# Where the weight sums of a gated feed-forward stage stand in VectorE's queue

## The chip, the cores and the metric

The kernel runs on one core of a Trainium2 chip. The metric is the device time of one execution in microseconds: 1489.54 us before the change, the median of three runs (1488.31 to 1489.56). The profiled execution has a span of 1488.6 us, with the TensorE clock granted in full.

## What is computed

Four layers on a sequence of 2048 tokens of width 1024: linear attention, gated feed-forward, and both once more with the same weights, each behind a layer norm and with a residual. The change lies in the feed-forward layer:

```python
x = x + _A_ref(_layernorm(x), A_wqkv, A_wo)              # linear attention, 32 heads
x = x + _B_ref(_layernorm(x), B_W_gate, B_W_up, B_W_down)
# _B_ref:
gate = einsum("bsd,df->bsf", x, W_gate)                  # d = 1024, f = 3584
up = einsum("bsd,df->bsf", x, W_up)
gate = gate * (gate > 0)
return einsum("bsf,fd->bsd", gate * up, W_down)
```

## The kernel before

The attention layers are `layer_A` (l = 0 and 2), the feed-forward layers `layer_B` (l = 1 and 3). A feed-forward layer goes over two chunks c of 1024 tokens. In each chunk, 14 units u (256 of the 3584 hidden columns) pass through `glu`, and then `down` multiplies the hidden tiles by W_down.

`glu` forms the gate and up products of a unit as 2 x 2 blocks with seven block products where eight would be needed. The price of that is sums of blocks: of the tokens (`sums_x`) and of the weights (`make_gu`, lines 680, 682 and 683: one instruction of 128 x 1024 and two of 128 x 512 for each of gate and up, so six for a unit). Both are formed on VectorE. A product (`mm`, line 742) is four matmuls into a PSUM bank; seven products for gate and seven for up make 56 matmuls a unit. Between them VectorE and ScalarE move partial results: v is product 5, copied by ScalarE to m5 (line 759); x is product 1, copied by ScalarE into y (line 763) and then completed by product 2; y takes product 6, is read by VectorE for z = y + m5 (line 773: zg and zu), takes product 7, is read again for m5 = y + m5 (line 776), and takes product 4. The matmuls that add to y must wait until VectorE has read it. The finished gate is clipped by ScalarE (line 750, r), and VectorE multiplies gate and up into the hidden tile h (`put`, line 753), three times a unit; GpSimd does the fourth product (line 780). The last of the three, h<-yu,r, is the last VectorE instruction of the unit's own, and `self.last_put` holds it.

The weight sums are made once, in chunk 0 of layer 1 (`first`), and written to memory (line 684, a DMA issued on ScalarE's queue) for the later three chunks, which load them (line 673). In this chunk, unit u's call in `layer_B` does this before `glu`: it lets the ring of weight tiles load up to five tiles ahead of unit u's gate weight (line 670, on SyncE's queue), and puts the sums of unit u+1 on the list of later tasks, due at the fourth tick, that is after four products of unit u. The sums of unit 0 are made in `layer_A`, near its end. All weight tiles, hidden tiles and token tiles share one pool of 16 slots, so a load may have to wait until an earlier weight tile has been used.

What order the instructions have on an engine is decided by the program order together with a scheduler, which may move an instruction ahead of others on its engine where its data allow it. `behind` limits that: with `self.tc.issue_after(it)` the instructions made inside stand after `it` in their engine's queue. This adds no semaphore. Before the change `it` is `self.last_x`, the last residual addition of the attention layer (line 564), which is long past; so all the sums may stand as early as the scheduler places them. In the built program they are mostly in groups of four weights (12 instructions), in every second unit.

Of the kernel before, what the change touches and what calls it, by code (L numbers as in the profile page):

```python
# [89 lines left out]
class _Net:  # L90
# [770 lines left out]
    def layer_B(self, l, final):  # L861
        ring = self.ring

        def behind(it, fn):
            with self.tc.issue_after(it.ins):
                fn()

        for c in range(2):
            hT = []
            first = l == 1 and c == 0  # L870
            for u in range(self.U):
                if u % 2 == 0:
                    hT.append(self.slot(f"h{l}_{c}_{u // 2}", dtype=F16))
                ring.load_to(ring.index((l, c, "g", u)) + 5)
                if first:
                    if u + 1 < self.U:
                        self.later.at(4, lambda u=u: behind(self.last_x, lambda: [
                            self.make_gu(ring.get((l, c, w, u + 1)), w, u + 1) for w in "gu"]))
                self.glu(l, c, u, hT)
                if c == 0 and u == (self.U - 1 if first else 0):  # L880
                    after = self.last_put.ins
            if c == 0:
                self.ln_chunk(l, 1, 20, 3, 3, after)
            elif not final:
                self.ln_later(l + 1, 0, 28, 6, 4)
            self.down(l, c, hT, final)
# [68 lines left out]
```

## Time and profile before

| stage or engine | figure |
|---|---|
| span of the profiled execution | 1488.6 us |
| first gated chunk: first product to first down product | 237.22 to 411.08 us |
| one undisturbed unit of it (unit 2: 262.08 to 274.17) | 12.09 us |
| TensorE matmul busy, whole span | 1474.4 us |
| VectorE busy, whole span | 836.7 us |
| VectorE busy, 297 to 309 us and 309 to 321 us | 9.65 and 5.46 us |
| weight sums: L680, L682, L683 (28 each), median | 682, 419, 418 ns |
| landing of a weight load (L670): least, median, most | 3.6, 4.9, 10.4 us |

In a timeline row the columns are start and duration in us, engine, line, operation, output<-input, shape, count, and in brackets how long the engine was idle before and what ended that. PE is TensorE, DVE is VectorE, ACT is ScalarE, POOL is GpSimd, SPq SyncE's queue. A row of a wait gives who waited for whom, the total in us, how often, and the longest. Matmul rows overlap: four matmuls are shown with 1.03 us, and follow each other at 0.864 us.

### The profile page before, as it was taken

How to read it: one execution, taken by the hardware profiler on the slowest of the kernel's cores; microseconds unless marked ns; L12 is line 12 of the kernel's file. 1: busy time of each engine (PE TensorE's matmuls, PEld its weight loads, DVE VectorE, ACT ScalarE, POOL GpSimd, SP SyncE). 2: the span in 40 equal slices, each digit the busy share in tenths (PEclk: the TensorE clock that was granted, in tenths of full speed). 3: DMA queues.
4: the chain of work that ended last, by engine and by line, in shares of the span. 5: the costliest groups of instructions: out<-in, count | busy, mean ns of one | idle time of the engine just before them, and what ended most of it. 6: DMA issues, size and time to landing. Idle time of an engine off the chain costs nothing.

```text
span 1488.6 us, 18556 instructions
## 1 busy us (share of the span) xinstructions
PE 1474.4 (99%) x6993; PEld 670.5 (45%) x7039; DVE 836.7 (56%) x1427; ACT 508.6 (34%) x911; POOL 277.1 (19%) x190
## 2 busy tenths in 40 slices
PE   9999999999999999999999999999999999999999
PEld 4444444444444444444444444444444444444444
DVE  8995789565494533346366555874345433444632
ACT  5752323333330233340057513333332203333300
POOL 1356540110000011110023492401111000111000
PEclk9999999999999999999999999999999999999999
DMA  9856539443458954445723038494343688444461
GB/s 282 215 167 177 114 60 260 155 170 127 145 174 230 344 179 130 150 133 189 221 43 71 29 52 253 87 283 142 129 151 132 188 240 276 142 142 143 150 209 43
DMA packets 313753, 242.91 MB, mean 163 GB/s; under 512 B 105280, under 2 KB 290880, under 8 KB 312768
## 3 DMA queue, kind: packets, MB, share of 16 engines
q1 hardware_dynamic: 303696, 221.41, 50.9%
q10 hardware_dynamic: 9968, 20.32, 3.6%
q8 instruction: 55, 0.90, 0.3%
q14 instruction: 34, 0.28, 0.1%
HBM read 186.65 MB, written 30.41 MB: 146 GB/s over the span
## 4 chain that ended last, share of the span: by engine, by line
PE 85%; DVE 5%; DMA 2%; issue 1%; ACT 0%; DVEq 0%
PE dy L826 10%; PE yu L742 10%; PE yg L742 10%; PE ps L430 8%; PE ps L465 7%; PE dv L826 6%; PE dx L826 6%; PE xu L742 6%; PE xg L742 6%; PE zu L742 3%; PE zg L742 3%; PE vu L742 3%; PE vg L742 3%; PE ps L557 2%; DVE x L564 1%; DVE stats L154 1%
## 5 line engine op out<-in xcount | busy, mean ns | idle before, releaser
L742 PEld LDWEIGHTS <-w 128*128 128x128 f16 (+1 forms) x3136 | 306.6, 98 | 375.8 <-issue 4.6
L430 PE MATMUL ps<-w,xnT 128*128 128x512 bf16 x1024 | 223.9, 379 | 0.5 <-DVE pq L380 0.2
L780 POOL TENSOR_TENSOR h<-m5u,m5g 128x512 f16<-128x512 f32 x56 | 71.2, 1271 | 815.4 <-DVE m5u L776 774.5
L826 PEld LDWEIGHTS <-h 128*128 128x128 f16 x1120 | 109.6, 98 | 132.2
L773 DVE TENSOR_TENSOR zg<-yg,m5g 128x512 f32<-128x512 f32 x56 | 39.1, 699 | 210.9 <-PE yg L742 210.9
L430 PEld LDWEIGHTS <-xnT 128*128 128x128 bf16 x1024 | 99.4, 98 | 120.9 <-issue 2.7
L742 PE MATMUL yg<-s,w 128*128 128x512 f16 x448 | 115.1, 379 | 3.6 <-DVE zg L773 3.6
L742 PE MATMUL xu<-xnT,w 128*128 128x512 f16 x448 | 115.0, 379 | 0.0
L742 PE MATMUL xg<-xnT,w 128*128 128x512 f16 x448 | 115.0, 379 | 0.0
L742 PE MATMUL yu<-s,w 128*128 128x512 f16 x448 | 115.0, 379 | 0.0
L557 PE MATMUL ps<-T,pqT 128*128 128x512 bf16 x500 | 110.4, 379 | 1.4 <-DVE x L564 0.8
L750 ACT ACTIVATE m5g<-m5g 128x512 f32<-128x512 f32 x56 | 35.3, 630 | 202.0 <-DVE m5g L776 187.6
L826 PE MATMUL dy<-w,h 128*128 128x512 f16 x448 | 98.0, 379 | 0.0
L826 PE MATMUL dx<-w,h 128*128 128x512 bf16 x436 | 96.7, 379 | 0.6
L511 POOL TENSOR_TENSOR kvc<-pq,kvc 128x1024 f32<-128x1024 bf16 x32 | 68.1, 2129 | 81.5 <-DVE den L516 70.4
L154 DVE BATCH_NORM_STATS2 stats<-x 128x6 f32<-128x512 f32 (+1 forms) x120 | 76.5, 672 | 1.9 <-DMA x<-in_A_x_dram 1.6
L557 PEld LDWEIGHTS <-pqT 128*128 128x128 bf16 x512 | 49.9, 98 | 61.4 <-issue 1.5
L161 ACT ACTIVATE rstd<-mv,eps 128x1 f32<-128x1 f32 x64 | 18.2, 290 | 163.2 <-DVE mv L159 163.1
L447 POOL TENSOR_TENSOR kvc<-kvc,slab 128x512 f32<-128x512 f32 x46 | 57.1, 1249 | 78.8 <-DVE slab L380 61.0
L759 ACT ACTIVATE m5g<-vg 128x512 f32<-128x512 f32 x56 | 33.4, 597 | 100.6 <-PE vg L742 73.9
L826 PEld LDWEIGHTS <-e 128*128 128x128 f16 x448 | 43.8, 98 | 52.9
L776 DVE TENSOR_TENSOR m5u<-yu,m5u 128x512 f32<-128x512 f32 x56 | 38.7, 691 | 50.7 <-PE yu L742 50.7
(105 smaller groups left out, 1941.0 us busy)
## 6 DMA issues: line engine op xcount, KB each, us to landing
w<-in_B_W_gate_dram SPq DMA_DIRECT2D x56, 512.0 KB, 6.0
w<-in_B_W_up_dram SPq DMA_DIRECT2D x56, 512.0 KB, 4.6
w<-td SPq DMA_DIRECT2D x32, 896.0 KB, 4.6
w<-in_B_W_down_dram SPq DMA_DIRECT2D x24, 896.0 KB, 5.1
w<-tg SPq DMA_DIRECT2D x42, 512.0 KB, 6.9
w<-tu SPq DMA_DIRECT2D x42, 512.0 KB, 6.0
w<-in_A_wqkv_dram SPq DMA_DIRECT2D x10, 1024.0 KB, 8.2
wd<-in_B_W_down_dram SPq DMA_DIRECT2D x7, 1024.0 KB, 7.2
```

What stands on the lines that cost most here:

```text
L154: self.nc.vector.bn_stats(out=stats[:, c, :], in_=src[:, c * fmax:(c + 1) * fmax])
L430: nc.tensor.matmul(by_row(ps), lhsT=self.xnT[l, l_q][:, kt, j * P:(j + 1) * P], rhs=w[:, kt, :].rearrange("p (b i d) -> p i b d", i=R, d=H ...
L447: nc.gpsimd.tensor_tensor(out=ksum[:, cols], in0=ksum[:, cols], in1=pk, op=ALU.add)
L465: nc.tensor.matmul(ps, lhsT=self.xn[l, t][:, d * P:(d + 1) * P], rhs=self.pk[l, t][:, h * NW:(h + 1) * NW], start=(t == 0), stop=(t == sel ...
L511: nc.gpsimd.tensor_tensor(out=prod, in0=pq_of[sc, j], in1=zrow, op=ALU.mult)
L557: nc.tensor.matmul(ps, lhsT=pqT[sc][:, g, j * P:(j + 1) * P], rhs=T[g // 4][:, g % 4, n2 * NW:(n2 + 1) * NW], start=(g == 0), stop=(g == G ...
L742: nc.tensor.matmul(ps, lhsT=W[w][m][:, k, :], rhs=A[m][:, k, :], start=start and k == 0, stop=k == 3, skip_group_check=True)
L750: nc.scalar.activation(out=out, in_=ps, func=ACT.Relu)
L773: nc.vector.tensor_tensor(out=Z[w], in0=Y[w], in1=V[w], op=ALU.add)
L776: nc.vector.tensor_tensor(out=V[w], in0=Y[w], in1=V[w], op=ALU.add)
L780: nc.gpsimd.tensor_tensor(out=h[:, 3, :], in0=V["u"], in1=V["g"], op=ALU.mult)
L826: nc.tensor.matmul(banks[j], lhsT=A(k)[:, j * P:(j + 1) * P], rhs=w[:, i, :], start=start and k == 0, stop=k == self.U - 1, skip_group_che ...
```

## The change

The sums of unit u+1 are placed behind the latest product `self.last_put` where there is one, instead of behind the attention layer's last addition. The name is looked up when the task runs, in unit u after four of its products, when the latest such product is the third of unit u-1 (h<-yu,r). For u = 0 there is none yet in this chunk, and the sums of unit 1 stay behind `last_x`. It is meant to keep VectorE's queue from being filled with sums that are not yet needed.

```diff
                 if first:
                     if u + 1 < self.U:
-                        self.later.at(4, lambda u=u: behind(self.last_x, lambda: [
+                        self.later.at(4, lambda u=u: behind(self.last_put if u else self.last_x, lambda: [
                             self.make_gu(ring.get((l, c, w, u + 1)), w, u + 1) for w in "gu"]))
```

## The prediction

> **What bounds the kernel now.** I read the page first. TensorE is busy for 1474.4 of 1488.6 us, so nothing but TensorE's order and its gaps can move the end.
>
> ```profile
> PE 1474.4 (99%) x6993; PEld 670.5 (45%) x7039; DVE 836.7 (56%) x1427; ACT 508.6 (34%) x911; POOL 277.1 (19%) x190
> ```
>
> The changed lines belong to one stage, the first gated chunk. Its first product starts at 237.22 us and the down product's first (dx) at 411.08. I asked that stage for its waits, TensorE first and then VectorE (columns: engine, line, releaser, us in total, times, longest).
>
> ```profile
> PE yg L742 <- DVE zg L773: 3.6, 2, 2.1
> PE vg L742 <- DVE w L680: 0.2, 1, 0.2
> ```
>
> ```profile
> DVE w L680 <- DMA w<-in_B_W_gate_dram: 4.1, 2, 2.4
> DVE w L680 <- DMA w<-in_B_W_up_dram: 2.8, 2, 1.9
> ```
>
> TensorE waits twice for VectorE's zg, and VectorE itself sat waiting for weight loads in front of its weight sums. The timeline of unit 11 (units counted from 0) shows how the two hang together:
>
> ```profile
> 371.88 0.37 SPq L670 DMA_DIRECT2D w<-in_B_W_gate_dram  x1
> 372.74 0.37 SPq L670 DMA_DIRECT2D w<-in_B_W_up_dram  x1
> ...
> 375.96 0.69 DVE L680 TENSOR_TENSOR w<-w 128x1024 f16<-128x1024 bf16 x1 [2.38 <-DMA w<-in_B_W_gate_dram]
> ...
> 378.59 1.03 PE L742 MATMUL yu<-s,w 128*128 128x512 f16 x4
> 379.45 0.69 DVE L680 TENSOR_TENSOR w<-w 128x1024 f16<-128x1024 bf16 x1 [1.88 <-DMA w<-in_B_W_up_dram]
> 380.18 0.43 DVE L682 TENSOR_TENSOR w<-w 128x512 f16<-128x512 bf16 x1
> 380.64 0.43 DVE L683 TENSOR_TENSOR w<-w 128x512 f16<-128x512 bf16 x1
> 380.98 0.69 DVE L773 TENSOR_TENSOR zg<-yg,m5g 128x512 f32<-128x512 f32 x1
> ...
> 381.73 0.81 PE L742 MATMUL yg<-s,w 128*128 128x512 f16 x3 [2.11 <-DVE zg L773]
> ```
>
> The sums at 375.96 and 379.45 are those of unit 13, two units ahead of use; their weights were asked for only at 371.88 and 372.74, when unit 10 gave its slots back. zg of unit 11 stands behind them in VectorE's queue. It was ready at about 378 and ran at 380.98, and the next matmul of yg, which overwrites what zg reads, waited. Unit 9 has the same picture: the sums of unit 12 run at 353.22, zg at 354.75, yg at 355.50.
>
> [...] zg waited behind a sum that it does not need. [...] at 371.70 an L682 took 0.83 us beside GpSimd's 1.27 us product at 370.98, against a median of 419 ns. [...] 682 ns for 1024 elements, against 0.69 for 512 out of PSUM. Since the trace has all durations, I use its own.
>
> **The change, part by part.** Nothing is added or removed: 84 sum instructions (L680, L682, L683, 28 each) and 28 write-backs (L684) stay. What moves is the place on VectorE of the sums of units 2 to 13. Each block of six now stands after the product h<-yu,r (put 2) of the unit two before it, and so before zg of the unit one before it. In the built order of the changed kernel the blocks are one per unit, where they were mostly four weights in a row every second unit. No semaphore is added: in the built program the first sum waits for its load alone, and order in the queue does the rest. What is queued behind a block is zg, and TensorE's yg waits for zg; so I cost the block against that gap.
>
> First, the room. Take unit 2, which has no sums in its first half:
>
> ```profile
> 262.08 1.03 PE L742 MATMUL vg<-s,w 128*128 128x512 f16 x4
> 262.35 0.69 DVE L753 TENSOR_TENSOR h<-yu,r 128x512 f16<-128x512 f32 x1 [1.03 <-PE yu L742]
> ...
> 267.53 0.70 DVE L773 TENSOR_TENSOR zg<-yg,m5g 128x512 f32<-128x512 f32 x1 [4.49 <-PE yg L742]
> ```
>
> VectorE is idle for 4.49 us, from 263.04 to 267.53. The block needs, from the medians of the tile view,
>
> ```profile
> L680 DVE TENSOR_TENSOR w<-w x28: 677/682/1096, 238.6 to 379.5; 128x1024 f16<-128x1024 bf16 x28
> ```
>
> 2 x 0.68 + 4 x 0.42 = 3.04 us. That fits with 1.4 us to spare. With the longest durations seen (L680 1.10, L682 0.84, L683 0.43) it is 2 x (1.10 + 0.84 + 0.43) = 4.74 us, 0.25 late; but zg then ends at about 268.5 and yg is not due before 268.99. So the upper bound is hidden too. Besides, GpSimd's product (260.53 to 261.80 here) is over by then, so I take the median.
>
> Second, whether the weights are there. The block of unit u+1 now runs about 1 us after unit u starts. Units 10 to 12 are the tight ones. The last weights of unit 12 are asked for at 360.87, those of unit 13 at 372.74; less the gain below, 359.2 and 371.1. Unit 11 starts at 372.55 and unit 12 at about 387.1; less the gain, 370.9 and 383.0. Adding 1 us, the lead is 12.7 and 12.9 us. The landing times of L670 are 3.6/4.9/10.4 (least, median, most). Hence no block should wait for a load.
>
> Third, write-backs. L684 issues on ScalarE's queue and stands between m5u and yu there, waiting for L683 of the gate weight. Counting from a unit's start: put 2 ends at 0.96, two L680, two L682 and one L683 bring 3.6 at the latest, the issue itself 0.33, so 3.9. ScalarE's yu<-xu was at 265.74, or 3.66. It slips by up to 0.3 us; the matmul that needs it, xu's second pass, is at 5.18, yu's at 6.05. Cost 0. A write-back now lands some ten us into the unit before its slot's last use, a whole unit before the next load wants the slot. Cost 0. Two loads (w16, w17) no longer wait for a write-back and may start some 6 us earlier, at 237 to 239; nothing needs them before unit 2. Cost 0. One matmul of the next unit's vg is placed inside every unit instead of some; its sum and bank are ready 3 us before. Cost 0.
>
> Now what goes away. Four matmuls of a product take 0.864 us in the chain of waits. Unit 9: yu at 352.95 + 0.864 = 353.81, yg at 355.50, a gap of 1.69. Unit 11: 378.59 + 0.864 = 379.45 to 381.73, a gap of 2.28. Unit 0 has a small one: the sums of unit 2's gate weight push m5g (L776) to 245.81, and yg goes on at 246.55 instead of 246.31; with m5g ready at about 245.65, some 0.17 comes back. Sum: 1.69 + 2.28 + 0.17 = 4.14 us. As a check, 14 units of 12.09 us (262.08 to 274.17) are 169.3, the stage takes 173.86, so 4.6 us is all that can be had; the 0.4 left is unit 0's own first sums, whose place does not change. After the stage the built orders agree, and its triggers hang on TensorE, so the shift should reach the end whole: 1489.54 - 4.14 = 1485.40 us.
>
> **Rivals.** (a) Half: the stall of unit 11 returns because unit 13's loads land late, or a block's tail delays zg a little. For it: DMA was busy 0.54 to 0.75 in those windows. Against: the 12 us of lead. Time 1489.54 - 1.69 - 0.17 = 1487.7. (b) No change: the 4 us come back as waits in the down product or the second chunk, whose loads have slots freed in the same order. Against: after 411 us TensorE's matmuls wait for 0.7 us in all, and the loads shift with the stage. Time 1489.5. (c) Slower: the blocks are in front of zg in twelve units. If each ran d longer than the room, the time is 1489.5 - 4.1 + 12 d; d = 0.6 gives 1492.6. [...] Against: the room is 1.4 us and a further 0.7 before yg is due.
>
> **How the numbers follow.** Forecast 0.82, (a) 0.07, (b) 0.07, (c) 0.04. The limits of 0.2% are 1486.6 and 1492.5. The forecast's time is uncertain by the 0.4 us of unit 0 and the 1.3 us between the runs of before, so it lies at 1484 to 1486.5 and counts as faster; (a) and (b) are within 0.2%. Faster 0.82, same 0.14, slower 0.04. The range runs from 1484.0 to 1487.7, which takes in (a) and leaves out (b), (c) and a little below.
>
> **What would show it.** Right: in the changed trace L680's waits for DMA and the two waits of yg for zg are gone, a block of six follows each h<-yu,r and ends about 1.4 us before zg, and dx starts near 406.9. Wrong: new waits of yg for zg in many units (c), an L680 still waiting for a load at unit 12 (a), or dx at 407 and new TensorE waits later (b).

## The result, and the profile after

The changed kernel takes 1485.78 us (median of six runs, 1484.59 to 1486.82). The kernel before takes 1489.71 us (median of six, the three named above and three more, 1488.31 to 1490.74). The ratio is 0.9973, with a 95% interval of 0.9961 to 0.9986, so the difference is clear of the noise. The forecast was 1485.40 us, and faster by its limit of 0.2%. The measured difference is 0.27%, with an interval of 0.14 to 0.39%.

On the page, TensorE is busy for almost as long as before, in a span of 1483.6 us where it was 1488.6:

```profile
PE 1473.4 (99%) x6993; PEld 670.5 (45%) x7039; DVE 833.1 (56%) x1427; ACT 508.8 (34%) x911; POOL 276.6 (19%) x190
```

These are the waits of TensorE in the first gated chunk (engine, line, releaser, us in total, times, longest). Of the two rows of before only the small one is left:

```profile
PE vg L742 <- DVE w L680: 0.2, 1, 0.2
```

VectorE's waits in that chunk follow. Before, there were two rows in which L680 waited for a DMA, 6.9 us together. There is none now. VectorE's zg waits for TensorE in 13 of 14 units; before, it did so in 10:

```profile
DVE zg L773 <- PE yg L742: 32.3, 10, 4.5
```

And after:

```profile
DVE zg L773 <- PE yg L742: 25.3, 13, 4.3
DVE h L753 <- PE yu L742: 13.8, 14, 1.0
```

The timeline of unit 11, the place of the longer stall before, now reads:

```profile
369.54 0.37 SPq L670 DMA_DIRECT2D w<-in_B_W_gate_dram  x1
370.40 0.37 SPq L670 DMA_DIRECT2D w<-in_B_W_up_dram  x1
370.48 0.69 DVE L753 TENSOR_TENSOR h<-yu,r 128x512 f16<-128x512 f32 x1 [1.03 <-PE yu L742]
...
371.09 1.28 DVE L680 TENSOR_TENSOR w<-w 128x1024 f16<-128x1024 bf16 x2
...
372.29 0.75 DVE L682 TENSOR_TENSOR w<-w 128x512 f16<-128x512 bf16 x2
...
372.96 0.75 DVE L683 TENSOR_TENSOR w<-w 128x512 f16<-128x512 bf16 x2
...
373.78 0.58 ACT L763 ACTIVATE yu<-xu 128x512 f32<-128x512 f32 x1 [0.40 <-DVE w L683]
...
375.44 0.70 DVE L773 TENSOR_TENSOR zg<-yg,m5g 128x512 f32<-128x512 f32 x1 [1.73 <-PE yg L742]
376.25 1.03 PE L742 MATMUL yu<-s,w 128*128 128x512 f16 x4
...
377.12 1.03 PE L742 MATMUL yg<-s,w 128*128 128x512 f16 x4
```

The loads at 369.54 and 370.40 are those of unit 13, asked for, as before, when unit 10 gave its slots back. But the six sums at 371.09 to 373.71 are now those of unit 12, whose weights were asked for a unit earlier. VectorE then sits idle for 1.73 us until TensorE has filled yg, zg runs at 375.44, and the next yg follows yu at 377.12, one product (0.87 us) later, without a gap. Unit 9 has the same picture, with zg at 351.27 and yg at 352.94.

The first down product, dx, starts here:

```profile
406.25 2.11 PE L826 MATMUL dx<-w,h 128*128 128x512 bf16 x8
```

The first product of the stage is at 236.50, so the stage takes 169.75 us, where it took 411.08 - 237.22 = 173.86: 4.11 us less. What else differs between the two profiles lies outside: 0.72 us ahead of the stage, where the code is the same, and 0.17 us behind it (1077.52 us to the end of the span before, 1077.35 after).

### The profile page after: what moved, and what is told of

The parts are those of the page before. It is cut to its first block, busy times and chain, and to the rows that moved or that the text cites. A ratio compares the mean times of both kernels' runs of the same rounds, so it can differ in the third digit from the quotient of the medians.

```text
span 1483.6 us, 18555 instructions
## 1 busy us (share of the span) xinstructions
PE 1473.4 (99%) x6993; PEld 670.5 (45%) x7039; DVE 833.1 (56%) x1427; ACT 508.8 (34%) x911; POOL 276.6 (19%) x190
## 4 chain that ended last, share of the span: by engine, by line
PE 93%; DVE 4%; DMA 1%; issue 1%; ACT 0%; SPq 0%; DVEq 0%
PE ps L430 15%; PE yg L742 10%; PE dy L826 10%; PE yu L742 10%; PE ps L465 7%; PE dv L826 6%; PE dx L826 6%; PE xg L742 6%; PE xu L742 6%; PE vg L742 3%; PE vu L742 3%; PE zu L742 3%; PE zg L742 3%; PE ps L557 2%; DVE x L564 1%; DVE stats L154 1%
## 5 line engine op out<-in xcount | busy, mean ns | idle before, releaser
L753 DVE TENSOR_TENSOR h<-yu,r 128x512 f16<-128x512 f32 x56 | 38.7, 691 | 55.9 <-PE yu L742 55.9
```

The costliest lines, as they stand in the source:

```text
L753: self.last_put = nc.vector.tensor_tensor(out=h[:, b, :], in0=ps, in1=R.pop(b), op=ALU.mult)
```

## Experiments

"Stage" below is the time from the first product of the first gated chunk to its first dx, in the profiled execution. Ratios are to the kernel before, timed in the same series of runs. The diffs show only the parts of the lines that change.

**Which units pay: the late ones.** The stalls stood in units 9 and 11, in front of which the sums of units 12 and 13 waited for loads. So only those two blocks were moved, in units 11 and 12 of the loop:

```diff
-    behind(self.last_x, lambda: [
+    behind(self.last_put if u >= 11 else self.last_x, lambda: [
```

> Only the sums of units 12 and 13 stand behind the latest gate-up product; those of units 2 to 11 stay in early groups. Theory (two stalls of TensorE, caused by late loads in front of zg in units 9 and 11): nearly all of the gain, 1.69 + 2.28 = 4.0 us below before, no wait of yg for zg. Rival (the gain comes from spreading the sums over all units, off GpSimd's product): two units of twelve, at most 0.7 us below before.

Measured: 1486.5 us, ratio 0.998 (0.9973 to 0.9987); stage 169.91 us. TensorE's waits in the stage, and the one DMA wait that VectorE has left:

```profile
PE vg L742 <- DVE w L680: 0.2, 1, 0.2
```

```profile
DVE w L680 <- DMA w<-in_B_W_up_dram: 1.1, 1, 1.1
```

Two blocks out of twelve bring 3.95 of the 4.11 us of the stage. The remaining DMA wait stands in unit 9, at 350.44 us. The zg behind it still has 0.42 us of idle time, so this late load costs nothing.

**The complement: the early ones alone.** The same line with `0 < u < 9`, so that the sums of units 2 to 9 stand in their new place and those of 10 to 13 in their old one:

```diff
-    behind(self.last_x, lambda: [
+    behind(self.last_put if 0 < u < 9 else self.last_x, lambda: [
```

> The reverse: the sums of units 2 to 9 stand behind the latest gate-up product, those of units 10 to 13 stay where the scheduler puts them, with the gate weight of unit 12 before zg of unit 9 and both weights of unit 13 before zg of unit 11. Theory: both stalls stay, 0.2 us below before from unit 0 alone. Rival (spreading): eight units of twelve, about 2.7 us below before.

Measured: 1490.58 us, ratio 0.9999 (0.999 to 1.0008): no gain that the noise leaves visible, and not the 2.7 us of the rival. Seven of its 13 runs had a mean granted TensorE clock below 1.000, 0.998 or 0.999 (more on this below). The other six have a median 1.1 us below that of the runs of before at full clock. The stage takes 172.55 us, and both stalls are there, somewhat shorter than in the profile of before:

```profile
PE yg L742 <- DVE zg L773: 2.5, 2, 1.7
```

The timeline of its unit 11 has the picture of before:

```profile
374.02 0.69 DVE L680 TENSOR_TENSOR w<-w 128x1024 f16<-128x1024 bf16 x1 [2.41 <-DMA w<-in_B_W_gate_dram]
...
377.09 0.69 DVE L680 TENSOR_TENSOR w<-w 128x1024 f16<-128x1024 bf16 x1 [1.46 <-DMA w<-in_B_W_up_dram]
...
378.62 0.69 DVE L773 TENSOR_TENSOR zg<-yg,m5g 128x512 f32<-128x512 f32 x1
...
379.37 1.02 PE L742 MATMUL yg<-s,w 128*128 128x512 f16 x4 [1.73 <-DVE zg L773]
```

**One block alone.** With `self.last_put if u == 12 else self.last_x` only the sums of unit 13 move:

```diff
-    behind(self.last_x, lambda: [
+    behind(self.last_put if u == 12 else self.last_x, lambda: [
```

> Only the sums of unit 13 stand behind the latest product. Theory: the stall of unit 11 goes, that of unit 9 stays: 2.28 us below before, one wait of yg for zg of 1.5 us left. Rival (spreading): 0.3 us below before.

Measured: 1487.18 us, ratio 0.9982 (0.9975 to 0.9988); stage 170.90. The stall of unit 11 is gone, that of unit 9 stays, at 354.19 us, and only half as long as in the profile of before:

```profile
PE yg L742 <- DVE zg L773: 0.8, 1, 0.8
```

So the stall of unit 11 goes with the block of unit 13 alone.

**The place, one unit earlier.** Is it enough that the sums stand behind some product? Here they stand behind h<-yu,r of one unit earlier (`puts` keeps each unit's last product):

```diff
-    behind(self.last_x, lambda: [
+    behind(self.puts[-2] if u > 1 else self.last_x, lambda: [
...
+    if first:
+        self.puts.append(self.last_put)
```

> Every block of sums may stand one unit earlier, behind the third product of unit u-2 instead of u-1. In the built order both weights of unit 13 are then again before zg of unit 11, while no weight of unit 12 is before zg of unit 9. Theory (what counts is the lead of the load over the sums, not that there is an order): the stall of unit 11 comes back with about 2.3 us, that of unit 9 stays away: 1.7 us below before. Rival (any order that keeps sums from piling up is enough): the full 4 us below before.

Measured: 1488.57 us, ratio 0.9994 (0.9986 to 1.0002); stage 171.70. In the built order the six sums of unit 13 then stand in front of the zg of unit 11 again, and there the stall is back. No sum of unit 12 stands in front of the zg of unit 9, and that stall is gone. TensorE's and VectorE's waits in the stage:

```profile
PE yg L742 <- DVE zg L773: 1.6, 1, 1.6
```

```profile
DVE w L680 <- DMA w<-in_B_W_gate_dram: 2.3, 1, 2.3
DVE w L680 <- DMA w<-in_B_W_up_dram: 2.0, 2, 1.4
```

So what counts is the distance between the load's issue and the place of the sums in the queue. With one unit less, the loads of unit 13 are late again.

**Is it the landing, or only the work in front of zg?** In the kernel before, the sums of units 12 and 13 were made to read the gate and up weights of units 11 and 12, which have long landed. The right sums of these two units are left out. The number of sums stays: 12 between the zg of unit 8 and that of unit 9, and 9 between those of units 10 and 11, as in the kernel before. The scheduler places some of them a little earlier (two of the six of unit 13 stand ahead of h<-yu,r, where all six stood behind it):

```diff
-    raw, T = self.raw_gu(t), self.sums_gu(t)
+    raw, T = self.raw_gu(other if other is not None else t), self.sums_gu(t)
...
-    self.make_gu(ring.get((l, c, w, u + 1)), w, u + 1)
+    self.make_gu(ring.get((l, c, w, u + 1)), w, u + 1, ring.get((l, c, w, u)) if u >= 11 else None)
```

> The kernel before, with its early blocks, but the sums of units 12 and 13 read the weights of units 11 and 12, which have long landed (so the sums of these two units are left out and others formed in their place; the loads are still made, and the slots are still waited for). The number of sums in front of zg in units 9 and 11 stays. Theory (the landing of a late load holds the queue): both stalls go, 4.0 us below before. Rival (it is the amount of work in front of zg): both stalls stay, time as before.

Measured: 1486.16 us, ratio 0.997 (0.9962 to 0.9978); stage 169.90, all but 0.15 us of the change's gain, with the old grouping. The sums of unit 13 still stand in front of the zg of unit 11, but they run from 369.13 to 372.96, and zg has room again:

```profile
372.54 0.42 DVE L683 TENSOR_TENSOR w<-w,w 128x512 f16<-128x512 bf16 x1
...
375.46 0.70 DVE L773 TENSOR_TENSOR zg<-yg,m5g 128x512 f32<-128x512 f32 x1 [2.50 <-PE yg L742]
```

This settles the cause: it is not the amount of VectorE's work in front of zg, but a sum at the head of the queue that waits for its load. The slightly earlier places do not change that, as zg has 2.50 us to spare.

**How much room the new place has.** In the kernel after, the sums of units 2 to 13 are made twice, and in another run three times, with the same values:

```diff
+    for _ in range(2 if u > 1 else 1):      # 3 in the other run
         v.tensor_tensor(out=T[:, 0:2, :, :], ...)
         v.tensor_tensor(out=T[:, 2, :, :], ...)
         v.tensor_tensor(out=T[:, 3, :, :], ...)
```

> The changed kernel with the sums of units 2 to 13 made twice over, the same values again. In the built order 11 of the 12 instructions stand before zg. From the changed kernel's trace six take 2.62 us, so 11 take about 4.9; from 1.1 us after the unit's start they end at 6.0, zg at 6.75, and yg is due at 7.1. Theory: no wait of TensorE, time as the changed kernel, within 0.5 us. Rival (the room is only the 1.73 us of idle before zg): zg is 0.6 us late in 12 units, and TensorE with it: 7 us above the changed kernel.

> The same, three times over; 16 of 18 instructions stand before zg. They end at about 8.3 us into the unit, zg at 9.0, yg due at 7.1: TensorE waits about 1.9 us in each of 12 units, 23 us above the changed kernel. VectorE's work in a unit is then 7.9 + 4.8 = 12.7 us against 12.1 of TensorE. Rival (write-backs and loads of this stage set its time): unchanged.

Measured, twice: 1485.12 us, ratio 0.9966 (0.9954 to 0.9977), stage 169.76 us, the same as after. Twelve sums in each of twelve units cost nothing. In its unit 2 the idle time ahead of zg is used up, and one sum is left over behind zg (line numbers are one higher in this kernel):

```profile
265.86 0.42 DVE L683 TENSOR_TENSOR w<-w 128x512 f16<-128x512 bf16 x1
266.20 0.69 DVE L774 TENSOR_TENSOR zg<-yg,m5g 128x512 f32<-128x512 f32 x1
266.80 0.41 DVE L684 TENSOR_TENSOR w<-w 128x512 f16<-128x512 bf16 x1
```

Measured, three times: 1506.8 us, ratio 1.0107 (1.0087 to 1.0127), stage 191.28 us: 21.5 more than after, about the size that was expected, 23. But it does not stall where that was expected. TensorE's waits name the sums themselves and not zg:

```profile
PE vu L743 <- DVE w L681: 10.0, 11, 0.9
PE vg L743 <- DVE w L681: 7.4, 12, 0.7
```

The products vg and vu of the next unit, which read these sums, are placed inside the running unit, in front of yg. So the first to be late is the consumer of the sums, not the neighbour in the queue. The room is therefore somewhere between one more set of sums and two. The place is not the only limit here. VectorE is then busy for most of the time (start:end, length, busy and count, granted clock, DMA share, GB/s):

```profile
300.00:328.00 28.00, 24.13 (x51) 1.00 0.39 132
```

That is about 12.1 us for each unit of 14.04 us (zg at 299.65 and 313.69), as much as TensorE needs for an undisturbed unit (12.09). The run doesn't tell the two limits apart.

**The rest of unit 0.** The stage of the kernel after is 169.75 us, and 14 undisturbed units would be 169.3. The rest was put down to the sums of unit 0. To get it, those were put three ticks earlier in the attention layer, in the kernel after:

```diff
-    later.at(8, lambda w=w: self.make_gu(ring.get((last_ln, 0, w, 0)), w, 0))
+    later.at(5, lambda w=w: self.make_gu(ring.get((last_ln, 0, w, 0)), w, 0))
```

> The changed kernel with the sums of unit 0 due three ticks earlier (at 5 instead of 8), inside the attention layer's last quarter. Theory: the wait of vg for L680 at the start of the stage goes, 0.4 us below the changed kernel in the stage, too little for the times to show. Rival: the 3 us block in front of L564 makes the attention layer's PSUM banks late and costs TensorE 1 us or more there.

Measured: 1487.9 us, ratio 0.9987 (0.998 to 0.9995), and a stage of 173.11 us, 3.4 more than after. Both expectations missed. In the timeline the weight sums are early, but now stand ahead of the token sums (L715, L716), which the first vg needs too:

```profile
237.10 0.42 DVE L682 TENSOR_TENSOR w<-w 128x512 f16<-128x512 bf16 x1
237.56 0.42 DVE L683 TENSOR_TENSOR w<-w 128x512 f16<-128x512 bf16 x1
...
239.10 0.42 DVE L715 TENSOR_TENSOR s<-xnT 128x512 f16<-128x512 f16 x1
...
239.57 1.04 PE L742 MATMUL vg<-s,w 128*128 128x512 f16 x4 [2.04 <-DVE s L715]
```

Again a neighbour in the queue pays, this time 2.04 us, though no load is late. The other part was a surprise. It shows in the windows view of TensorE (columns as above; the granted clock is a share of full speed):

```profile
238.00:240.00 2.00, 0.42 (x2) 1.00 1.07 252
240.00:241.00 1.00, 1.00 (x5) 0.78 0.90 265
241.00:242.00 1.00, 1.00 (x3) 0.50 1.10 407
242.00:243.00 1.00, 1.00 (x4) 0.50 1.05 406
243.00:244.00 1.00, 1.00 (x4) 0.51 1.04 386
244.00:246.00 2.00, 2.00 (x10) 1.00 1.13 336
```

After the gap the granted clock is about 0.50 for some 3.5 us. From 200 to 240 us and from 244 to 250 us it is 1.00. The loss is 0.22 + 0.50 + 0.50 + 0.49 = 1.7 us, about what this profile's mean clock of 0.999 stands for (0.001 of 1487.5 us is 1.5 us). With the 2.04 us that is 3.7 us, where the stage lost 3.4; the old waits of unit 0 that are gone go the other way.

**Does a gap on TensorE cost granted clock as well?** Each run comes with the mean granted clock of its execution, to three places. In the kernel before, 38 of 146 runs in the four series of these experiments are below 1.000, mostly at 0.999. In the kernels where yg waits for no zg (after, its late part alone, landed weights, sums twice) it is none of 50. As 0.001 of 1488 us is 1.5 us, a mean of 0.999 fits one such spell. To make gaps of known length, VectorE's zg of unit 11 was made 5, 7 and 10 times in the kernel after:

```diff
+    for _ in range(5 if (l, c, u, w) == (1, 0, 11, "g") else 1):     # 7, 10
         nc.vector.tensor_tensor(out=Z[w], in0=Y[w], in1=V[w], op=ALU.add)
```

> The kernel after, with the zg sum of unit 11 made five times in place of once (the same values). In the trace of after its zg ends 0.98 us before the TensorE product yg that waits for it is due; four more at some 0.65 us are 2.6 us, so a gap of about 1.6 us opens in front of yg at 377.1 us, about the size of the one in unit 9 of the kernel before. Theory (a short gap sometimes costs granted clock too): time 1485.8 + 1.6 = 1487.4 us in runs with a mean granted clock of 1.000, and some runs, one in five or fewer, at .999 and some 1.5 to 2 us longer. Rival (a gap costs its own length only): all runs near 1487.4 us and at 1.000.

> As the run before, with the zg sum of unit 11 made seven times: a gap of about 2.9 us, longer than either gap of the kernel before. Theory: most runs or all at a mean clock of .999, the granted clock at about half for some 3 us after the gap in the profiled run, time 1485.8 + 2.9 + 1.5 = 1490.2 us. Rival: 1488.7 us at 1.000.

> As the runs before, with the zg sum of unit 11 made ten times: a gap of about 4.9 us. Theory: every run at .999, half clock for some 3 us after the gap in the profiled run, time 1485.8 + 4.9 + 1.5 = 1492.2 us; were the loss in clock to grow with the gap, more than that. Rival: 1490.7 us at 1.000.

Measured: 1485.37 us (ratio 0.9974, 0.9965 to 0.9983), 1486.08 us (0.9981, 0.9974 to 0.9987) and 1488.51 us (0.9995, 0.9987 to 1.0003), at a clock of 1.000 in all 44 runs. The gaps did not come out as meant. Given more work on VectorE, the scheduler placed other matmuls in front of yg, and the time was paid in smaller pieces. TensorE's waits with ten zg:

```profile
PE xg L742 <- ACT yg L763: 1.7, 1, 1.7
PE yg L742 <- DVE zg L774: 1.0, 1, 1.0
```

With seven there is one of 0.8 us, with five none. So these runs are no test of gaps above 1.7 us. The third adds that waits of up to 1.7 us left the clock at 1.000 in 13 runs, which is little: in the same series the kernel before was below 1.000 in only 4 of 38.

The early-units kernel, of which 7 of 13 runs were below 1.000, was profiled a second time to see where its clock falls:

> The kernel with the new place for the sums of units 2 to 9 only, profiled once more, since 7 of its 13 timed runs had a mean granted clock of .999 or .998 and its first profile had 1.000. Theory (a gap of about 2 us sometimes costs clock): with a mean clock of .999 in the profiled run, the granted clock in 2 us windows is 1.00 up to the late zg of unit 11 and about 0.5 in some 3 us right after its gap of 1.6 to 2.2 us, near 380 us, and nowhere else in the stage. Rival (the lower clock comes from elsewhere): it falls at another place. With 1.000 in the profiled run it tells nothing of the place.

Measured: 1488.73 us, ratio 0.9996 (0.9986 to 1.0007), stage 172.32; two of its ten runs at 0.999, the profiled one at 1.000. So it tells nothing of the place, which was seen once only, in the kernel with unit 0's sums earlier.

## Why the prediction was right

The mechanism was right: both stalls were late loads in front of zg, and they are gone. Taken together, the stages show it to a few hundredths of a microsecond. The waits of yg for zg, from each profile, account for nearly all the differences:

| kernel | stage, us | waits of yg for zg, us | stage less waits, us |
|---|---|---|---|
| before | 173.86 | 1.52 + 2.11 | 170.23 |
| early units only | 172.55 | 0.76 + 1.73 | 170.06 |
| the same, second profile | 172.32 | 0.65 + 1.60 | 170.07 |
| one unit earlier | 171.70 | 1.64 | 170.06 |
| unit 13 only | 170.90 | 0.83 | 170.07 |
| units 12 and 13 | 169.91 | none | 169.91 |
| old order, landed weights | 169.90 | none | 169.90 |
| after | 169.75 | none | 169.75 |
| after, sums twice | 169.76 | none | 169.76 |

What is left in the last column has two known parts. Each wait is 0.17 us shorter in the profile than the gap between the products (1.52 and 2.11 against the 1.69 and 2.28 of the prediction). And the small stall of unit 0, 0.15 us, is left in the kernels that do not move the sums of unit 2: before, one unit earlier, unit 13 only, units 12 and 13, and landed weights.

Point by point, by the steps of the prediction:

- **What goes away.** 4.14 us was worked out, 4.11 measured in the profiles. Both stalls are gone, and most of the small one of unit 0: TensorE's product zg starts at 244.73 and takes 0.864 us, to 245.59, and yg follows at 245.68. That is a gap of 0.09 us instead of 0.24.
- **The room.** Right in its verdict, off in its size, on the safe side. The block was costed at 3.04 us, the sum of six medians. It takes 2.62 us (371.09 to 373.71): two sums of one shape in a row show 1.28 and 0.75 us together, less than twice the 0.68 and 0.42 of one, so the records of neighbours overlap. The idle time before zg is 1.73 us, not 1.4. The long durations of the upper bound no longer occur at all:

```profile
L680 DVE TENSOR_TENSOR w<-w x28: 681/682/685, 237.9 to 383.8; 128x1024 f16<-128x1024 bf16 x28
```

  Before, its longest was 1096 ns. The reason given was that GpSimd's product is over when the block starts. In unit 11 of after it ends at 369.9, before 371.09. That this overlap made the outliers was argued, not tested.
- **Whether the weights are there.** No L680 waits for a load. The load of unit 13's up weights at 370.40 and their sums from 383.17 on are 12.8 us apart, as predicted (12.7 and 12.9). With one unit less, the wait is back (2.3 us, the run one unit earlier).
- **Write-backs.** ScalarE's yu slipped as foreseen, but by less: 0.13 us in unit 11 (0.40 us of idle time ahead of it, which the profile puts down to L683, instead of 0.27), where up to 0.3 was allowed. Nothing waits for it.
- **The stage's end and what follows.** dx starts at 406.25, not at the forecast 411.08 - 4.14 = 406.94. The 0.69 us between them were there before the stage began (0.72), in code that is the same. After the stage nothing was given back, so rival (b) falls.
- **Rivals (a) and (c).** (a) appears only when the block stands a unit earlier. (c) needs d above zero in many units. The sums made twice show that there is room for another whole block, so a single block was far from that. With the sums made three times a cost in every unit did become real, 1.8 us in each of twelve (21.5 / 12), but by way of vg and vu rather than zg.

What the prediction did not have is that the stalls differ from execution to execution. They were 3.63 us in the profile of before, and 2.49 and 2.25 us in the two of the early-units kernel, which leaves those two blocks where they were. So the profile that the forecast was worked out from had long stalls. The runs at a clock of 1.000 say the same: the kernels without the two stalls have medians only 2.6 to 3.6 us below those of before in their own series (2.6 with landed weights, 2.7 for units 12 and 13, 3.6 with the sums twice; why these differ by 1 us is open). Against that stands a cost that the prediction put at nothing, the clock: in the four series the medians of before at 1.000 are 1488.7 to 1489.2 us, and at 0.999 they are 1491.0 to 1491.5. The measured difference of 3.93 us may hold both, and how it divides between them can't be had from six runs. That it came so near to 4.14 us is therefore in part luck.

## What to carry to other kernels

In a queue, look for the instruction that waits for a DMA and then for what stands behind it. Here the cost was that of the neighbour, not of the instruction that waits. Before, zg of unit 11 stood behind sums that waited 2.38 and 1.88 us for their loads, and yg came 2.28 us late. With only units 12 and 13 moved, a sum waited 1.1 us and no product was late for it. Work that is prepared ahead should be placed late enough that its data has landed even in a bad case. It should also be early enough that its own consumer, and not only the next instruction in the queue, is on time. Here the first took one unit (12 us against landings of up to 10.4 us), and the second had room for one more set of sums. When a stall depends on a landing time, take its size from more than one profile.

## What the runs showed of the hardware

In one profiled execution a gap on TensorE was followed by a loss beyond its own length. In that of unit 0's sums earlier, a gap of 2.04 us was followed by some 3.5 us at a granted clock of about 0.50, a further 1.7 us. There the weight loads of single matmuls are 0.43 us apart (rows of 241.18, 241.61, 242.04 us), twice the 0.216 us at which undisturbed matmuls follow each other. The DMA traffic of that moment (386 to 407 GB/s) is not enough to explain it, since the profile of before has as much with the clock at 1.00:

```profile
242.00:243.00 1.00, 1.00 (x6) 1.00 1.03 406
```

It doesn't happen each time: the profiled execution of before has a gap of 2.11 us with a mean clock of 1.000, and of 1.00 in every 2 us from 378 to 388 us, around that gap. The table says how many runs of each kernel were below 1.000. The first four kernels have a wait of 1.6 us or more in front of yg or vg in their profiles:

| kernel | runs | below 1.000 | median at 1.000, us | median at 0.999, us |
|---|---|---|---|---|
| before, four series | 146 | 38 | 1488.7 to 1489.2 | 1491.0 to 1491.5 |
| early units only, two series | 23 | 9 | 1488.09; 1488.55 | 1491.11; 1491.60 |
| one unit earlier | 13 | 3 | 1488.38 | 1490.37 |
| unit 0's sums earlier | 22 | 8 | 1487.51 | 1489.32 |
| no wait there, or waits up to 0.9 us | 75 | 0 | | |
| zg made 5 and 7 times: waits up to 0.8 us | 31 | 0 | | |
| zg made 10 times: waits up to 1.7 us | 13 | 0 | | |

The fifth row takes in after, its late part alone, unit 13 alone, landed weights, and sums twice and three times. The medians at 0.999 lie 1.8 to 3.1 us above those at 1.000. So the lower clock goes with the long waits, in kernels timed side by side, except that the kernel with zg made 10 times, with its wait of 1.7 us, has none of 13. That it falls right behind them was seen in one profile, and is not shown for the others.

Two things are left open: the shortest gap behind which the clock falls (the attempt at gaps of set length gave waits of 1.7 us at most), and where in the kernel before the clock falls, since neither its profile nor the two of the early-units kernel caught it.
